# Decode attention with a gated unit: loading Wq as 16 partitions and then 112, instead of a quarter of every partition's rows and then the rest

## The chip, the cores and the metric

The kernel runs on one core of a Trainium2 chip. The metric is the device time of one execution in microseconds, and the number that counts is the median of several runs. One more execution was taken with the hardware profiler; it has a span (first to last recorded instruction) and a device time of its own that is a little longer than the span.

## The reference, cut to what matters

Everything is bfloat16 in memory. There are 8 sequences of one new token each (B = 8, D = 512), 32 query heads, 8 key/value heads of 128 elements, and a cache of 8192 positions of which the last W = 2048 are attended to.

```python
xn = layernorm(x)                                  # (8, 1, 512)
q  = (xn @ wq)                                     # wq: (512, 4096) -> 32 heads x 128
k  = k_cache[:, :, Sk - W:, :]                     # (8, 8, 2048, 128), each head for 4 q heads
v  = v_cache[:, :, Sk - W:, :]
p  = softmax(q . k * 128 ** -0.5)
s  = (p . v) @ wo                                  # wo: (4096, 512)
h  = sigmoid(xn @ w_gate) * (xn @ w_up)            # w_gate, w_up: (512, 1792)
g  = silu(h @ w_down)                              # w_down: (1792, 512)
return x + s * g
```

The windows of K and V are 4 MB for each sequence, Wq and Wo are 4 MB each, and the three matrices of the gated unit are 1.75 MB each: some 81 MB are read and 8 KB written.

## The kernel before, in words

Every large operand is loaded into a ring of five buffers of 32 KB per partition (`ring_tile`), each of which holds one 4 MB operand. The loads stand in a list, `loads`, in the order Wq, K0, K1, K2, V0, then K and V alternating, then the gate and up matrices, the down matrix, and Wo. `issue_loads` takes loads off the list while `free_bufs` says that a buffer is free. All of them are issued from SyncE (SP). The first five are issued at once; each later one is issued where the program has read a buffer out, and waits on SP until that is so. The order of all other work is written out by hand (`manual_schedule`), and each engine follows it.

Wq is seen as 128 partitions of KT = 4 rows: partition p holds rows 4p to 4p + 3, each 4096 elements (8 KB), so that a partition's 32 KB lie in one piece in memory and in the buffer. `load_wq` (lines 96 to 103) issues two loads at line 101.

Meanwhile x is loaded from ScalarE's queue, normalised on VectorE and transposed into `xnT_sb`. The q matmuls (line 303) go over the halves s, then over kt, then over four column strips a:

```python
for kt in range(KT):
    for a in range(QP):
        nc.tensor.matmul(q_ps[PW * a : PW * (a + 1), :],
                         lhsT=xnT_sb[:, kt, :],
                         rhs=w_tiles["q"][:, kt, o : o + rep * Dh], ...
```

Each contracts over all 128 partitions of Wq. VectorE copies the result to `qx_sb` (L313) and transposes it (L322), TensorE spreads it (L330), ScalarE copies it to `qc_sb` (L338), and `q_fill` (L349) puts 16 small copies per sequence into the operand `qz`. When q has been read out of Wq, that buffer is handed to the load of K3.

For each sequence b, VectorE transposes the K tile in four turns (`k_turn`, L371), TensorE makes the scores (`qk`, L388), and the softmax and the product with V follow one or two sequences later (L401 to L544). The gated unit and the product with Wo (L668) stand at the end, Wo in seven loads that grow smaller so that little is left to do after the last one.

## Time and profile before

| | |
|---|---|
| median of 3 runs | 197.53 us (197.53 to 197.66) |
| the profiled execution: device time | 197.59 us |
| the profiled execution: span | 195.8 us |
| PE matmul busy | 114.0 us (58%), 1092 instructions |
| DVE busy | 116.8 us (60%), 170 instructions |
| ACT busy | 38.7 us (20%), 112 instructions |
| POOL busy | 7.5 us (4%), 27 instructions |
| loads on the one queue | 6368 packets, 81.01 MB, 97.3% of 16 engines' span |
| HBM reads over the span | 414 GB/s |
| from issue to landing: first piece of Wq, second piece | 4.8 us, 11.6 us |
| from issue to landing: K, V (median) | 29.4 us, 24.1 us |
| mean granted TensorE clock | 0.808 |

The busy times of the compute engines are sums over the span; the line for loads is the time that packets took on the 16 DMA engines together. "Issue to landing" counts from the instruction on SP to the completion of the whole load, and so takes in the time that the load stands behind others in the queue.

### The profile page before, as it was taken

The page shows a single profiled execution, that of the slowest core. Times are in us where ns is not written, and L with a number is a line of the kernel's source. Part 1 is how long each engine was busy: PE and PEld are TensorE (multiplying, and loading weights), DVE is VectorE, ACT ScalarE, POOL GpSimd, SP SyncE. Part 2 cuts the span into 40 slices and gives each one's busy share as a digit, 9 for nine tenths or more (in the row PEclk, how much of TensorE's full clock was granted, in tenths as well). Part 3 has the DMA queues.
Part 4 walks back from the last instruction along what each step waited for, and adds up shares of the span by engine and source line. Part 5 has one row for each costly group of instructions (what it writes and reads, how often), then busy time and mean ns, then how long its engine had stood idle before and what let it go on. Part 6 is the DMA issues. An engine that isn't in the chain of part 4 may idle for free.

```text
span 195.8 us, 2620 instructions
## 1 busy us (share of the span) xinstructions
PE 114.0 (58%) x1092; PEld 47.6 (24%) x1092; DVE 116.8 (60%) x170; ACT 38.7 (20%) x112; POOL 7.5 (4%) x27
## 2 busy tenths in 40 slices
PE   0133025709709970799059923990796099687562
PEld 0011001102103240214021311160225025463461
DVE  2304498299398449944895479739936952454101
ACT  1102910015015011501141003211501110225000
POOL 2480000000000000000000000000000000000000
PEclk9999555855975998599958995798599579969699
DMA  6999999999999999999999999999999999999991
GB/s 241 457 402 432 429 442 432 432 429 429 429 429 429 429 432 437 425 424 429 432 435 429 429 435 439 432 429 425 432 429 432 425 429 439 422 428 426 421 398 39
DMA packets 6410, 81.17 MB, mean 415 GB/s; under 512 B 1000, under 2 KB 1024, under 8 KB 1408
## 3 DMA queue, kind: packets, MB, share of 16 engines
q1 hardware_dynamic: 6368, 81.01, 97.3%
q8 instruction: 8, 0.13, 0.2%
q10 hardware_dynamic: 32, 0.01, 0.0%
q14 instruction: 2, 0.02, 0.0%
HBM read 81.01 MB, written 0.01 MB: 414 GB/s over the span
## 4 chain that ended last, share of the span: by engine, by line
DMA 33%; PE 32%; DVE 30%; issue 1%; ACT 1%; SPq 1%; DVEq 0%
PE s_ps L388 24%; DVE k_sb L371 24%; DMA wo_sb<-in_A_wo_dram 11%; DMA v_sb<-in_A_v_cache_dram 11%; DMA k_sb<-in_A_k_cache_dram 11%; PE o_ps L493 6%; DVE o_r L514 2%; DVE pt_bf L433 2%; PE o_ps L522 1%; DVE o_sb L544 1%; ACT o_r L510 1%; DVE o_q L535 1%; DVE mx L401 1%; SPq L101 0%; PE pc_ps L439 0%
## 5 line engine op out<-in xcount | busy, mean ns | idle before, releaser
L371 DVE STREAM_TRANSPOSE k_sb<-k_sb 128x2048 uint32<-128x2048 uint32 x32 | 72.9, 2292 | 6.1 <-DMA k_sb<-in_A_k_cache_dram 6.0
L388 PE MATMUL s_ps<-k_sb,qz 128*32 128x512 bf16 x256 | 61.7, 1086 | 11.7 <-DVE k_sb L371 11.6
L439 PE MATMUL pc_ps<-pt_bf,spr 128*32 128x128 bf16 x128 | 4.7, 292 | 40.8 <-DVE pt_bf L433 40.8
L401 DVE TENSOR_REDUCE mx<-s_ps 128x1 f32<-128x512 f32 x8 | 5.5, 692 | 28.7 <-PE s_ps L388 28.7
L493 PE MATMUL o_ps<-v_sb,pT_sb 128*32 128x256 bf16 (+1 forms) x416 | 22.0, 310 | 0.0
L388 PEld LDWEIGHTS <-qz 128*32 128x32 bf16 x256 | 10.0, 114 | 48.7 <-issue 48.6
L493 PEld LDWEIGHTS <-pT_sb 128*32 128x32 bf16 (+1 forms) x416 | 14.7, 105 | 14.7 <-issue 9.7
L349 ACT COPY qz<-qc_sb 32x64 bf16<-32x64 bf16 x64 | 16.5, 303 | 0.7
L510 ACT ACTIVATE o_r<-o_ps,Cm 128x128 f32<-128x128 f32 x16 | 5.9, 368 | 53.3 <-PE o_ps L493 53.3
L514 DVE SCALAR_TENSOR_TENSOR o_r<-o_ps,Cm,o_r 128x128 f32<-128x128 f32 x28 | 9.7, 350 | 10.6 <-ACT o_r L510 10.2
L420 ACT ACTIVATE p_bf<-s_ps,nm 128x512 bf16<-128x512 f32 x8 | 5.5, 687 | 49.8 <-DVE nm L417 49.8
L439 PEld LDWEIGHTS <-spr 128*32 128x32 bf16 x128 | 3.4, 121 | 41.5 <-issue 40.9
L522 PE MATMUL o_ps<-o_r,rows 128*128 128x128 f32 x32 | 7.9, 339 | 4.8 <-DVE o_r L514 4.8
L475 DVE TENSOR_SCALAR pT_sb<-pc_bf,quarter 128x512 bf16<-128x512 bf16 x32 | 9.0, 350 | 0.2 <-ACT pc_bf L449 0.2
L449 ACT CAST pc_bf<-pc_ps 128x512 bf16<-128x512 f32 x8 | 4.7, 586 | 20.3 <-PE pc_ps L439 20.3
L303 PE MATMUL q_ps<-wq_sb,xnT_sb 128*32 128x512 bf16 x32 | 3.7, 611 | 5.4 <-DMA wq_sb<-in_A_wq_dram 5.0
L522 PEld LDWEIGHTS o_ps<-o_r,rows 128*128 128x128 f32 x32 | 5.1, 206 | 6.7 <-DVE o_r L514 6.7
L668 PE MATMUL a_ps<-wo_sb,o_sb 128*32 128x128 bf16 x128 | 4.7, 222 | 2.7 <-DMA wo_sb<-in_A_wo_dram 2.6
L433 DVE STREAM_TRANSPOSE pt_bf<-p_bf 128x512 bf16<-128x512 bf16 x8 | 5.4, 675 | 0.9 <-ACT p_bf L420 0.9
L535 DVE SCALAR_TENSOR_TENSOR o_q<-o_ps,rden,block 128x128 f32<-128x128 f32 x8 | 2.8, 351 | 5.2 <-PE o_ps L522 5.2
L313 DVE CAST qx_sb<-q_ps 128x256 bf16<-128x256 f32 x4 | 1.5, 420 | 7.0 <-PE q_ps L303 7.0
L668 PEld LDWEIGHTS <-o_sb 128*32 128x32 bf16 x128 | 4.0, 98 | 3.8 <-issue 3.7
(62 smaller groups left out, 54.6 us busy)
## 6 DMA issues: line engine op xcount, KB each, us to landing
k_sb<-in_A_k_cache_dram SPq DMA_DIRECT2D x8, 4096.0 KB, 29.4
v_sb<-in_A_v_cache_dram SPq DMA_DIRECT2D x7, 4096.0 KB, 24.1
v_sb<-in_A_v_cache_dram SPq DMA_DIRECT2D x2, 2048.0 KB, 19.9
wq_sb<-in_A_wq_dram SPq DMA_DIRECT2D x1, 3072.0 KB, 11.6
wgu_sb<-in_B_w_gate_dram SPq DMA_DIRECT2D x1, 1792.0 KB, 25.1
wgu_sb<-in_B_w_up_dram SPq DMA_DIRECT2D x1, 1792.0 KB, 28.9
wd_sb<-in_B_w_down_dram SPq DMA_DIRECT2D x1, 1792.0 KB
wo_sb<-in_A_wo_dram SPq DMA_DIRECT2D x1, 1408.0 KB
```

The lines of the kernel that those rows point to most:

```text
L349: nc.scalar.copy(out=z[rows, GL * gg : GL * (gg + 1), :, c0 : c0 + rep], in_=qc_sb[rows, :, gg, :, :, b].rearrange("p gl r we -> p gl we r"),)
L371: nc.vector.transpose(out=words, in_=words)
L388: nc.tensor.matmul(s_tiles[b][PW * gl : PW * (gl + 1), :], lhsT=qz[b % 2][:, h, we, :], rhs=kv[:, gg, gl, we // 2, we % 2], start=(we == 0 ...
L401: nc.vector.reduce_max(out=mx[:], in_=s_tiles[b][:], axis=AX.X)
L433: nc.vector.transpose(out=pt_bf[:].rearrange("p c g a r -> p (c g a r)"), in_=p_bf[:])
L439: nc.tensor.matmul(pc_ps[PW * a : PW * (a + 1), cl], lhsT=spr[:, cl].rearrange("k p gl -> k (p gl)"), rhs=pt_bf[:, :, :, a, :], start=True ...
L475: nc.vector.tensor_scalar(out=pT[:, :, :, gl, :], in0=pc[:].rearrange("p c g r -> p g c r"), scalar1=quarter[:, gl : gl + 1], scalar2=None ...
L493: nc.tensor.matmul(o_ps[rows * cg : rows * (cg + 1), :], lhsT=pT_tiles[b][:, gg, nch * m : nch * (m + 1)].rearrange("p c g r -> p (c g r)" ...
L510: nc.scalar.activation(out=o_r[:], in_=o_ps[:, 0:Dh], func=AF.Copy, scale=cm[:, 0:1])
L514: nc.vector.scalar_tensor_tensor(out=o_r[:], in0=o_ps[:, Dh * c : Dh * (c + 1)], scalar=cm[:, c : c + 1], in1=o_r[:], op0=ALU.mult, op1=AL ...
L522: nc.tensor.matmul(o2_ps[:], lhsT=rows128[gg][:].rearrange("p gl g r q -> p (gl g r q)"), rhs=o_r[:], start=(gg == 0), stop=(gg == NG - 1),)
L668: nc.tensor.matmul(a_ps[s][32 * c : 32 * (c + 1), :], lhsT=o2_sb[:, m, :], rhs=w_tiles["o"][:, m, DC * c + HC * s : DC * c + HC * (s + 1)] ...
```

## The change

Wq is still loaded by two loads from SP, in front of all others. Before, the first load brought row kt = 0 of every partition (128 packets of 8 KB, 1 MB in all) and the second rows 1 to 3 (128 packets of 24 KB, 3 MB). Now the first brings all four rows of partitions 0 to 15 (16 packets of 32 KB, 512 KB) and the second all four rows of partitions 16 to 127 (112 packets of 32 KB, 3.5 MB). Nothing else differs: all engines have the same instructions in the same order, two lines further up in the file after this place.

```diff
         src = A_wq.rearrange("(p kt) n -> p kt n", kt=KT)
-        for k0, k1 in ((0, 1), (1, KT)):
-            nc.sync.dma_start(
-                out=w_tiles["q"][:, k0:k1, :], in_=src[:, k0:k1, :]
-            )
+        for p0, p1 in ((0, 16), (16, P)):
+            nc.sync.dma_start(out=w_tiles["q"][p0:p1], in_=src[p0:p1])
```

## The prediction

> **What bounds the kernel now.** I read the page's slices first, then the queue totals, the chain in order of time, and last the first 32 us by timeline and by quarter-microsecond windows. From the page, the 40 slices of 4.9 us (busy tenths of the 16 DMA engines, then what they moved) and the queue that carries the loads (packets, MB, share of 16 engines' span):

> ```profile
> DMA  6999999999999999999999999999999999999991
> GB/s 241 457 402 432 429 442 432 432 429 429 429 429 429 429 432 437 425 424 429 432 435 429 429 435 439 432 429 425 432 429 432 425 429 439 422 428 426 421 398 39
> ...
> q1 hardware_dynamic: 6368, 81.01, 97.3%
> ```

> All loads go through one queue, and apart from the first slice and the last it never runs dry: 81.01 MB at some 430 GB/s is 188 us of a 195.8 us span. From the chain in order of time (start us, us, what), its first and last parts:

> ```profile
> 1.20 0.41 SPq L101
> 1.60 0.05 issue
> 1.66 20.83 DMA k_sb<-in_A_k_cache_dram
> ...
> 147.15 0.55 SPq L114
> 147.69 0.05 issue
> 147.75 22.01 DMA v_sb<-in_A_v_cache_dram
> 169.75 0.02 issue
> 169.77 22.31 DMA wo_sb<-in_A_wo_dram
> 192.08 0.04 issue
> ```

> The chain passes through DVE and PE between these, but the last V loads land 22 us after their issue: about 9.5 MB go through the queue in that time, their own 2 MB among them. So the engines of the core follow the stream, and its end follows its own bytes. Time lost on the DMA engines near the start is lost at the end, to the full amount; a delay off that stream costs nothing until its slack is used up.

> The start, in windows (us, busy time of PE, PEld, DVE, ACT, POOL, granted clock, DMA share, GB/s):

> ```profile
> 1.50:1.75 0.25, 0.00 (x0) 0.00 (x0) 0.00 (x0) 0.00 (x0) 0.25 (x2) 1.00 0.09 29
> 1.75:2.00 0.25, 0.00 (x0) 0.00 (x0) 0.00 (x0) 0.00 (x0) 0.13 (x1) 1.00 1.95 299
> 2.00:2.25 0.25, 0.00 (x0) 0.00 (x0) 0.00 (x0) 0.00 (x0) 0.00 (x0) 1.00 1.01 164
> 2.25:2.50 0.25, 0.00 (x0) 0.00 (x0) 0.00 (x0) 0.00 (x0) 0.00 (x0) 1.00 0.43 164
> 2.50:2.75 0.25, 0.00 (x0) 0.00 (x0) 0.02 (x1) 0.00 (x0) 0.00 (x0) 1.00 0.61 197
> 2.75:3.00 0.25, 0.00 (x0) 0.00 (x0) 0.25 (x1) 0.00 (x0) 0.00 (x0) 1.00 0.87 360
> 3.00:3.25 0.25, 0.00 (x0) 0.00 (x0) 0.22 (x2) 0.00 (x0) 0.00 (x0) 1.00 1.01 426
> ```

> Bytes flow 1 us after the first issue at 0.73 and reach full rate at 3.0. From 1.75 to 3.0 they come to (299 + 164 + 164 + 197 + 360) x 0.25 = 296 KB where 432 GB/s would have brought 540 KB: the slow start loses 0.56 us.

> **The change, part by part.** Bytes, issues and order are the same: two loads of Wq, then K0, K1, K2, V0. The packets differ: 128 of 8 KB and 128 of 24 KB become 16 of 32 KB and 112 of 32 KB. Per DMA engine that is one packet, then seven, instead of eight and eight. The unit: 432 GB/s (the rate between 40 and 80 us) over 16 engines is 27.0 GB/s for each, so a 32 KB packet takes 1.21 us.

> *The head of 16 partitions.* Every large load in the trace writes all 128 partitions, so the trace doesn't tell whether 27 GB/s is what one DMA engine sends or what one set of eight partitions can take. If only the engine limits, 512 KB takes 1.21 us and the head costs nothing. If the sets limit, 16 partitions reach at least two of the 16 sets: 54 GB/s, 9.7 us, which is 8.5 us more. With four sets it is 108 GB/s and 4.85 us, with eight 2.43 us. I take four: 4.85 us lies between the geometric (3.4) and the arithmetic middle (5.5) of the two ends. **Cost +3.64 us**, ends 0 and +8.5.

> [...]

> *The other 112 partitions.* Seven rows for each of 16 engines. The engines' own time is 7 x 1.21 = 8.5 us, the remaining seven eighths of Wq, so without meetings it costs nothing. But blocks of seven rows don't line up with sets of eight: where sets limit, two engines meet on one set at some steps and each takes double. Ends: no meetings, 0; a meeting at every step, +8.5 us. Since K0 lands when the slowest engine has delivered, and every later load gives each engine an equal share, the slowest engine's lag stays to the end. I take the middle, **+4.2 us**, for the row lies near neither end: engines start in step on blocks seven rows apart, then drift.

> *The slow start.* The worst windows still moved 164 to 197 GB/s, more than the 108 that the head can take, so the slow start now hides behind the head: **-0.56 us**. If it doesn't hide, 0.

> *The early matmuls.* Four q matmuls of kt=0 now run before the second piece lands; after the change every q matmul reads all 128 partitions and waits for both loads. The rows, from the timeline between 7 and 28 us (start us, us):

> ```profile
> 7.18 0.62 PE L303 MATMUL q_ps<-wq_sb,xnT_sb 128*32 128x512 bf16 x4 [0.34 <-DVE xnT_sb L205]
> ...
> 12.81 3.06 PE L303 MATMUL q_ps<-wq_sb,xnT_sb 128*32 128x512 bf16 x28 [5.01 <-DMA wq_sb<-in_A_wq_dram]
> ...
> 19.68 4.11 ACT L349 COPY qz<-qc_sb 32x64 bf16<-32x64 bf16 x16
> 22.51 6.70 DVE L371 STREAM_TRANSPOSE k_sb<-k_sb 128x2048 uint32<-128x2048 uint32 x3 [4.55 <-DMA k_sb<-in_A_k_cache_dram]
> ...
> 27.07 1.13 PE L388 MATMUL s_ps<-k_sb,qz 128*32 128x512 bf16 x4 [8.37 <-DVE k_sb L371]
> ```

> They put 0.62 us behind Wq's landing. The path from q ends with the copies into qz at 23.79, and the first matmul that reads them starts at 27.07, released by the transposes of K0: 3.28 us of slack. Wq and K0 are delayed alike, so the slack stays and the cost is **0**; without that cover it is 0.62 us.

> *SP.* Still two issues at L101, 0.41 us each; K0 to V0 queue behind them as now. The load of K3 waits until q has been read, issued at 15.91 now and at about 24 then. K0, K1, K2 and V0 (16.8 MB, 39 us) are queued ahead of it, so it stays covered. Later issues move with the landings. A lag of one engine by 4.2 us is within the shortest lead of the last loads (14.3 us from issue to landing), so no engine runs dry. **0**; nothing is late next but the stream.

> Sum: 3.64 + 4.2 - 0.56 = +7.3 us on the profiled execution's 197.59 us (span 195.8 and 1.8 around it; the median of the runs is 197.53): **204.9 us**.

> **The rivals.**

> *Head only.* The sets limit, but 112 rows flow as evenly as 128. For it: 112 rows still reach every set, and engines that fall out of step may stay out of each other's way. Against: blocks of seven and sets of eight share no alignment. 197.59 + 3.64 - 0.56 = 200.7 us.

> *Faster: only the engines limit.* The slow start is then a cost of the first packets: now 128 of 8 KB, each 32 KB from the next in Wq, then one run of 512 KB in 16 packets. For it: the loss sits wholly in the first 1.25 us, in which the first 8 KB packets flow. Against: a load on cold queues would begin as slowly with any packet, and then nothing changes. If the first 32 KB packets flow at 432 GB/s, 0.56 us goes: 197.0 us. It decides if the first piece lands under 1.8 us after its first byte.

> *Two sets.* Adjacent partitions share a set in blocks of eight: 197.59 + 8.5 + 4.2 - 0.56 = 209.7 us.

> *Strided rows.* If the 112 rows are dealt to the engines one by one, every step is again 16 adjacent rows: eight steps of +3.64, less 0.56, gives 226 us. For it: nothing in the trace tells how rows are dealt. Against: the even 430 GB/s of loads with eight rows per engine, which a deal of that kind couldn't reach if sets limit.

> **How the numbers follow.** Forecast 0.50; head only 0.24; engines only 0.12 (a gain 0.07, no difference 0.04, slightly slower 0.01); two sets 0.08; strided 0.06. A measurement of this kernel tells about 0.2% (0.4 us) from no change. The range runs from 200.0, below the head alone, to 210.0, above two sets; it leaves out engines only, strided, and the fringes. Faster 0.07, same 0.04, slower 0.89.

> **What would show it.** In the windows of the changed kernel, the DMA should move some 110 GB/s from about 1.75 to 6.5 us (full rate there would prove the head wrong), then below 430 until some 18 us. K0's first transpose should start near 30 instead of 22.51; a start near 26 means no meetings, one at 22 that only engines limit. From 40 us on the rate should be 430 again, with the last wo landing late by as much as K0. If K0 is late and the end isn't, the stream isn't the bound.

## The result and the profile after

The changed kernel takes 206.76 us (median of 5 runs, 206.49 to 206.96) against 197.59 us of the kernel before on the same chip: a ratio of 1.046, interval 1.045 to 1.047, or 9.2 us more. Its profiled execution took 206.77 us with a span of 205.0 us.

The slices of the profile's page are now 5.1 us long. These are the busy tenths of the 16 DMA engines, the rate, and the queue of the loads:

```profile
DMA  7999999999999999999999999999999999999991
GB/s 117 205 294 240 368 448 422 435 432 419 451 409 448 422 438 432 416 436 420 448 422 441 422 428 438 422 441 422 432 432 432 432 422 438 422 436 422 422 384 32
...
q1 hardware_dynamic: 6240, 81.01, 97.2%
```

The bytes are the same, with 128 packets fewer. The DMA engines count as busy from the first slice on, as before, but in the first five slices, some 25 us, they move far less. "Busy" here means that packets are open; the lower rate tells that each of them takes longer (2.17 us against 1.21, below). From the sixth slice on everything flows as before (409 to 451 GB/s up to the last two slices). The chain in order of time, its first and last parts:

```profile
1.18 0.40 SPq L101
1.58 0.05 issue
1.63 30.25 DMA k_sb<-in_A_k_cache_dram
...
177.51 23.15 DMA wo_sb<-in_A_wo_dram
200.66 0.04 issue
200.70 0.62 PE a_ps L666 x16
```

K0 lands after 30.25 us instead of 20.83, 9.4 us later, and the end moves nearly as much, by 9.2 us. The last row of the chain, the addition that makes y, before and after:

```profile
193.14 0.28 DVE y_bf L686
```

```profile
202.37 0.28 DVE y_bf L684
```

The DMA issues give the landing of the two pieces of Wq (KB, us from issue to landing); they were issued at 0.73 and 1.18:

```profile
wq_sb<-in_A_wq_dram SPq DMA_DIRECT2D x1, 3584.0 KB, 21.1
...
wq_sb<-in_A_wq_dram SPq DMA_DIRECT2D x1, 512.0 KB, 6.7
```

So the head lands at 7.4 us and the 112 other partitions at 22.3. The windows count a packet's bytes where the packet starts, so a short window is lumpy when packets last 2 to 4 us (801 GB/s from 1.50 to 2.00 us, 66 from 2.00 to 4.00). Here are two windows that hold several packets of each engine (start and end, length in us, busy times, granted clock, DMA share, GB/s):

```profile
8.20:20.00 11.80, 0.00 (x0) 0.00 (x0) 0.37 (x2) 0.00 (x0) 5.93 (x16) 1.00 1.00 261
24.00:32.00 8.00, 3.08 (x24) 0.99 (x17) 2.86 (x6) 2.93 (x10) 0.00 (x0) 1.00 1.01 434
```

The 112 partitions flow at 261 GB/s, K0 behind them at 434. In the packet records of the trace the 16 packets of the head take 3.1 to 4.0 us. Those of the 112 take a median of 2.17 us, where 1.21 us is the full rate. Taken in order of start as seven rounds of 16, they have medians of 2.73, 2.20, 1.75, 1.61, 2.03, 2.18 and 2.12 us, and not one packet takes less than 1.60: all engines are slow, not a few.

The path from q, from the timeline:

```profile
22.46 3.60 PE L301 MATMUL q_ps<-wq_sb,xnT_sb 128*32 128x512 bf16 x32 [15.23 <-DMA wq_sb<-in_A_wq_dram]
...
30.08 4.12 ACT L347 COPY qz<-qc_sb 32x64 bf16<-32x64 bf16 x16
31.90 8.89 DVE L369 STREAM_TRANSPOSE k_sb<-k_sb 128x2048 uint32<-128x2048 uint32 x4 [3.75 <-DMA k_sb<-in_A_k_cache_dram]
...
36.46 1.12 PE L386 MATMUL s_ps<-k_sb,qz 128*32 128x512 bf16 x4 [7.15 <-DVE k_sb L369]
```

All 32 q matmuls now wait for the second piece. The copies into qz end at 34.20 and the first matmul that reads them starts at 36.46. The transposes of K0 still release it, so 2.26 us of slack are left of 3.28.

### The profile page after: what moved, and what is told of

Same layout as the page of the kernel before. It is cut to its first block, busy times and chain, and to the rows that moved or that the text cites. A ratio compares the mean times of both kernels' runs of the same rounds, so it can differ in the third digit from the quotient of the medians.

```text
span 205.0 us, 2621 instructions
## 1 busy us (share of the span) xinstructions
PE 114.4 (56%) x1092; PEld 48.0 (23%) x1092; DVE 116.7 (57%) x170; ACT 38.6 (19%) x112; POOL 7.5 (4%) x27
## 3 DMA queue, kind: packets, MB, share of 16 engines
q1 hardware_dynamic: 6240, 81.01, 97.2%
HBM read 81.01 MB, written 0.01 MB: 395 GB/s over the span
## 4 chain that ended last, share of the span: by engine, by line
PE 36%; DVE 34%; DMA 26%; issue 1%; ACT 1%; SPq 1%; DVEq 0%
DVE k_sb L369 27%; PE s_ps L386 26%; DMA k_sb<-in_A_k_cache_dram 15%; DMA wo_sb<-in_A_wo_dram 11%; PE o_ps L491 8%; DVE pt_bf L431 2%; DVE o_r L512 2%; PE o_ps L520 1%; DVE o_sb L542 1%; ACT o_r L508 1%; DVE o_q L533 1%; DVE mx L399 1%; PE a_ps L666 1%; SPq L146 0%; SPq L101 0%
## 5 line engine op out<-in xcount | busy, mean ns | idle before, releaser
L491 PE MATMUL o_ps<-v_sb,pT_sb 128*32 128x256 bf16 (+1 forms) x416 | 23.2, 324 | 0.0
L386 PEld LDWEIGHTS <-qz 128*32 128x32 bf16 x256 | 10.5, 114 | 47.0 <-issue 46.9
L491 PEld LDWEIGHTS <-pT_sb 128*32 128x32 bf16 (+1 forms) x416 | 15.2, 109 | 15.1 <-issue 9.8
L311 DVE CAST qx_sb<-q_ps 128x256 bf16<-128x256 f32 x4 | 1.5, 420 | 16.8 <-PE q_ps L301 16.8
L336 ACT CAST qc_sb<-qr_ps 128x512 bf16<-128x512 f32 x2 | 1.1, 588 | 22.8 <-PE qr_ps L328 22.8
```

Of the source, the lines that this page charges most:

```text
L386: nc.tensor.matmul(s_tiles[b][PW * gl : PW * (gl + 1), :], lhsT=qz[b % 2][:, h, we, :], rhs=kv[:, gg, gl, we // 2, we % 2], start=(we == 0 ...
L491: nc.tensor.matmul(o_ps[rows * cg : rows * (cg + 1), :], lhsT=pT_tiles[b][:, gg, nch * m : nch * (m + 1)].rearrange("p c g r -> p (c g r)" ...
```

## Experiments

All experiments change `load_wq` alone; their times stand beside runs of the kernel before on the same chip (197.5 to 197.7 us).

### Which side is slow: the partitions written or the memory read

Theory S supposes that the partitions written share a limited way in, theory H that adjacent rows of memory share a limited way out. The changed kernel can't tell them apart, since its rows are adjacent on both sides. Four kernels load Wq in eight loads of 16 rows, adjacent or eight apart on either side. Where the two sides differ, rows land in other partitions than they should; the work stays the same:

```diff
-        for p0, p1 in ((0, 16), (16, P)):
-            nc.sync.dma_start(out=w_tiles["q"][p0:p1], in_=src[p0:p1])
+        far = src.rearrange("(j r) kt n -> r j kt n", r=8)
+        for r in range(8):
+            # e1: out [16 * r : 16 * (r + 1)], in src[16 * r : 16 * (r + 1)]
+            # e2: out [16 * r : 16 * (r + 1)], in far[r]
+            # e3: out [r : P : 8],             in src[16 * r : 16 * (r + 1)]
+            # e4: out [r : P : 8],             in src[r : P : 8]
```

> Wq comes in eight loads of 16 partitions; each writes 16 adjacent partitions and reads 16 adjacent rows of 32 KB of memory, as the changed kernel's first load does. In the changed kernel that load held the DMA engines for about 4 us (from 1.76 us to between 5 and 6.3) where 1.21 us was its share. Both theories expect eight times this: some 32 to 36 us for Wq instead of 9.7, and a time of 220 to 224 us. Theory S (the partitions written limit) and theory H (the memory read limits: adjacent rows of 32 KB lie in too few parts of it) differ only in the next three kernels. If instead the 4 us were a cost of the cold start, the other seven loads take 1.2 us each and the time is about 200 us.

> Eight loads of 16 adjacent partitions, but each reads 16 rows that lie 256 KB apart in memory, so the rows of Wq land in other partitions than they should (the output is not the reference's; the work is the same). Theory S: as slow as with adjacent rows, 220 to 224 us. Theory H: the reads are spread, the loads run at full rate, and the time is 197.5 to 198.5 us.

> Eight loads that read 16 adjacent rows each and write 16 partitions that lie eight apart (rows land in other partitions than they should, so the output is not the reference's). Theory S: partitions eight apart reach more sets; with eight sets a load takes 2.4 us, Wq 19.4 us, and the time is about 207 us; with all 16 sets 197.5 to 198.5. Theory H: 220 to 224 us, as with adjacent partitions.

> Eight loads of 16 partitions eight apart, from the rows of memory that belong to them, 256 KB apart. Theory S: the same time as with adjacent rows and partitions eight apart, about 207 us (eight sets). Theory H: 197.5 to 198.5 us.

| partitions written | rows read | time | one packet, median behind the first 16 |
|---|---|---|---|
| adjacent | adjacent | 223.9 us | 4.60 us |
| adjacent | eight apart | 223.0 us | 4.36 us |
| eight apart | adjacent | 208.2 us | 2.54 us |
| eight apart | eight apart | 208.3 us | 2.54 us |

Theory S holds in so far as the side written decides: the rows read change the time by under 1 us, the partitions written by 15 to 16. The window of the first kernel over five rounds of packets, and that of the third over seven:

```profile
9.90:32.90 23.00, 0.00 (x0) 0.00 (x0) 0.00 (x0) 0.00 (x0) 4.27 (x10) 1.00 1.01 114
```

```profile
4.00:21.60 17.60, 0.29 (x4) 0.31 (x5) 1.91 (x8) 1.35 (x2) 6.18 (x17) 1.00 1.01 209
```

Sixteen adjacent partitions take 114 GB/s, close to a quarter of 430, and partitions eight apart 209, close to half. The seven loads behind the first are as slow as was expected of the head (4.60 us a packet), so the head's loss isn't a cost of the cold start.

### One load, two halves, and the order

```diff
-        for p0, p1 in ((0, 16), (16, P)):
-            nc.sync.dma_start(out=w_tiles["q"][p0:p1], in_=src[p0:p1])
+        # e6: nc.sync.dma_start(out=w_tiles["q"], in_=src)
+        # e7: the loop over ((0, 64), (64, P))
+        # e8: the loop over ((0, 112), (112, P))
```

> Wq in one load of 128 partitions, 32 KB each. Theory S (the partitions reached by the engines at one time limit, not the size of a packet): full rate from the start, no head and no meetings, 197.0 to 197.8 us. If the slow start of the kernel before is a cost of its 8 KB packets, 197.0 to 197.2; if it is a cost of any first packet, 197.4 to 197.8. If 32 KB packets were slow in themselves, it would take 5 us or more longer.

> Wq as partitions 0 to 63 and then 64 to 127. By theory S each half reaches half of the 16 sets, two engines on each: packets of 2.3 to 2.5 us, Wq in about 20 us, a time of 207.5 to 208.5 us as with 16 partitions eight apart. If only loads of fewer rows than engines times two are slow, or engines take their rows so that they don't meet, 197.5 to 198 us.

> The two loads in the other order and at the other end: partitions 0 to 111 first, then 112 to 127. The sum of the two terms doesn't depend on the order: 206 to 207.5 us, with packets of about 2.1 us first and 16 packets of about 4.6 us behind them. If the loss of the 112 came from engines that left the head out of step, they flow at 1.2 us now, and the time is about 201 to 202 us.

One load of 128 packets of 32 KB takes 197.80 us, ratio to the kernel before 1.001 (1.0002 to 1.002), or 0.27 us more: the size of a packet costs next to nothing, and nothing is won either. Its window behind the first packets:

```profile
3.70:12.20 8.50, 0.29 (x4) 0.30 (x5) 1.92 (x8) 1.57 (x2) 4.91 (x16) 1.00 0.99 428
```

Packets behind the first 16 take 1.21 us, the first 16 a median of 1.90. So the slow start is there with large packets too, and the time is at the upper end of what was expected.

The halves take 208.4 us with packets of 2.56 us, as expected of two engines on each set. The other order, 112 before 16, takes 206.7 us, as much as the changed kernel. The landings (KB, us from issue to landing; issued at 0.73 and some 1.18):

```profile
wq_sb<-in_A_wq_dram SPq DMA_DIRECT2D x1, 3584.0 KB, 17.8
wq_sb<-in_A_wq_dram SPq DMA_DIRECT2D x1, 512.0 KB, 21.4
```

The 112 land at 18.5 and the 16 adjacent ones at 22.6, 4.1 us later. The packets of the 16 took 3.2 to 4.4 us, a little under the 4.6 expected; those of the 112 behind their first round took a median of 2.0 us. So the loss of the 112 is there without a head in front of them, and doesn't come from engines that left the head out of step.

### How the 112 rows are dealt to the engines

```diff
-        for p0, p1 in ((0, 16), (16, P)):
-            nc.sync.dma_start(out=w_tiles["q"][p0:p1], in_=src[p0:p1])
+        nc.sync.dma_start(out=w_tiles["q"][0:16], in_=src[0:16])
+        for j in range(7):
+            nc.sync.dma_start(out=w_tiles["q"][16 + j : P : 7], in_=src[16 + j : P : 7])
```

> The first load is the changed kernel's (16 adjacent partitions); the 112 others come in seven loads of 16 partitions that lie seven apart (16, 23, 30, ... then 17, 24, ...), one packet per DMA engine and load. That is the order in which the engines would work if the one load of 112 were dealt as a block of seven adjacent rows to each engine. Theory C (blocks of seven, whose meetings on a set cost the time): the same as the changed kernel, packets of about 2.1 us after the first, 206 to 207.5 us. Theory D (the 112 rows are dealt in another way): another time; if a load of 16 partitions seven apart meets no other on its sets, 1.2 us each and 201 us; if pairs meet all the time, 2.5 us each as with partitions eight apart, 209 to 210 us.

It took 207.0 us with a median packet of 2.19 us (2.17 in the changed kernel). Its window, beside the 261 GB/s of the changed kernel:

```profile
8.20:20.00 11.80, 0.00 (x0) 0.00 (x0) 0.45 (x3) 0.00 (x0) 6.01 (x17) 1.00 1.05 267
```

Its seven loads have median packets of 2.76, 2.24, 1.86, 1.75, 1.97, 2.22 and 2.13 us, nearly the rounds of the one load of 112. That is theory C: seven loads whose rows are placed by hand as blocks of seven do what the one load of 112 does. Dealing row by row, one of the rivals, is what the first kernel above does, and is far slower (223.9 us).

### Where a load of 64 partitions begins

If rows come in blocks, a load of 64 partitions gives engine e the partitions p0 + 4e to p0 + 4e + 3. Sliding p0 changes which partitions are written at the same time. By theory S two engines meet when the partitions that they write share a way in; which ones do, no run shows. "Coupled" below stands for the case that a meeting slows all 16 engines, not only those that meet.

```diff
-        for p0, p1 in ((0, 16), (16, P)):
+        # e9:  ((32, 96), (0, 32), (96, P))
+        # e10: ((28, 92), (0, 28), (92, P))
+        # e12: ((24, 88), (0, 24), (88, P))
+        # e11: ((16, 80), (0, 16), (80, P))
```

> Wq as partitions 32 to 95 first, then 0 to 31, then 96 to 127. With blocks of adjacent rows per DMA engine, the first load has engine e at partition 32 + 4e at its first step. [...] Wq in 4 x 1.2 + 4 x 2.5 = 15 us, a time of 202.5 to 203.5 us. Rival B (sets are eight adjacent partitions, with some other rate): 64 adjacent partitions reach eight sets wherever they begin, packets of 2.5 us, 208 to 209 us as with the halves.

> The same shifted by four: partitions 28 to 91 first, then 0 to 27 and 92 to 127. [...] The two loads behind it have 28 and 36 rows, which don't divide by 16, so the whole time says little: 205 to 213 us.

> Partitions 16 to 79 first, then 0 to 15, then 80 to 127. [...] Coupled: all packets of the first load take 2.2 to 2.5 us. [...] Behind it 16 adjacent partitions (4.6 us) and 48 in three packets of some 3 us: Wq in some 23 us and 209 to 212 us when coupled.

> Partitions 24 to 87 first, then 0 to 23 and 88 to 127. [...] The loads behind it have 24 and 40 rows, so the whole time says little: 208 to 216 us.

The middle 64 took 203.2 us, inside the 202.5 to 203.5 expected; that the first load would run at full rate was an assumption of the author's, which no run before it showed. Eight adjacent partitions as a set (208 us) are out. Here is the first load of each kernel, in a window behind its cold first packets, with the start at partition 32, 28, 24 and 16:

```profile
3.80:7.60 3.80, 0.29 (x4) 0.21 (x4) 1.74 (x8) 1.52 (x2) 0.38 (x3) 1.00 0.97 414
```

```profile
3.80:7.60 3.80, 0.29 (x4) 0.21 (x4) 1.74 (x8) 1.52 (x2) 0.38 (x3) 1.00 0.99 388
```

```profile
4.00:9.20 5.20, 0.29 (x4) 0.21 (x4) 1.92 (x8) 1.21 (x2) 1.97 (x9) 1.00 1.02 208
```

```profile
3.90:9.10 5.20, 0.29 (x4) 0.21 (x4) 1.92 (x8) 1.49 (x2) 1.70 (x7) 1.00 1.01 208
```

With the start at 28 most packets keep 1.21 to 1.25 us, and a few take 2.4 to 2.5, twice as long; the others aren't slowed with them. With the start at 24 all 16 engines take 2.5 to 2.6 us a packet, no less than at 16 or, in the halves, at 0. So in these kernels the cost doesn't grow step by step as the start moves down: it jumps between 28 and 24. Which engines meet in each of these loads, and how many, isn't shown.

The whole times (212.7, 217.7 and 214.4 us with the start at 28, 24 and 16) hold the loads behind, whose packets took up to 4.7 us. With the start at 28 and at 24 the engines also seem to have ended apart: the next to last slice fell to 296 and 269 GB/s, from 398 in the kernel before. What each of these adds isn't shown. At 24 and at 16 the time was above the 208 to 216 and 209 to 212 expected, at 16 because the 48 last partitions took some 3.9 us a packet and not 3.

Two things stay open. If the one load of 128 partitions gave each engine eight adjacent rows, its engines would write partitions eight apart at every step, as the loads of 16 partitions eight apart did at 209 GB/s, and yet it runs at 428. So either its rows are dealt in another way than those of 112 and 64, or the partitions written aren't all that counts; no run here takes that apart. And the third and fourth round of the 112 (medians 1.75 and 1.61 us) lie between the 1.21 us of full rate and the 2.5 to 2.6 of the slow first loads; why isn't shown.

## Why the prediction was right, and where it was not

It said 204.9 us (200 to 210); 206.76 came. The path, the head and the kind of loss of the 112 were as forecast; the size of one term was not. By its steps:

- **The bound.** Right. Lost DMA time goes to the end nearly in full: K0's first transpose is 9.4 us later (31.90 against 22.51, where a start near 30 was forecast), the final addition 9.2 us, and the queue holds 434 GB/s as soon as Wq is through.
- **The head, +3.64 less 0.56 for the hidden start.** Right, though "four sets" was picked as a middle between two ends and not read from a row, which is partly luck. With one load Wq lands at 13.0 us (12.3 after 0.73); seven rounds of 1.21 us back from there, its first round, slow start and all, landed at about 4.6 us. The head landed at 7.4: 2.9 us more, where 3.08 was forecast. Behind a warm queue a packet takes 4.60 us where four sets gave 4.85. Eight such loads at 3.39 us above the full rate, less 0.56 once, would come to 26.6 us; the first of the four kernels lost 26.3. How many sets 16 partitions reach, and that there are sets of eight at all, no run shows; what the runs show is 114 GB/s for 16 adjacent partitions, where four sets gave 108.
- **The 112, +4.2.** That they lose was right, and the blocks of seven placed by hand (2.19 us a packet against 2.17) fit the account of it; the size was not right. From 7.4 to 22.3 us is 14.9 us against 8.5: 6.4 us. The step that failed is the middle between "no meetings" and "a meeting at every step", and with it the notion that two engines that meet lose time, the slowest lags and the others run ahead. Not one of the 112 packets took less than 1.60 us, and in the first loads that begin at 24 and 16 all 16 engines take 2.5 to 2.6. So here the engines lose time together, and it is three quarters of the upper end (6.4 of 8.5 us). Which engines meet in which round isn't shown, so the single rounds (2.73 down to 1.61 us) and with them the account of the size stay in part open. The 2.2 us that the term lacked are most of the miss of the sum; the head's 0.2 us the other way leave some 1.9.
- **The slow start as a gain.** The rival on the faster side fell: one load with 32 KB packets starts as slowly and takes 197.80 us.
- **The early matmuls.** Cost 0, as forecast, but the slack didn't stay whole: 2.26 us of 3.28. Wq's second piece landed 9.5 us later and K0 9.4, and the head start of the four early matmuls was lost on top.
- **SP.** Right: K3 was issued at 26.11 us (about 24 forecast), and no slice behind shows a gap in the stream.
- **The other rivals.** Head only (200.7) fell with the 14.9 us that the 112 took. Two sets (209.7) fell with 4.60 us a packet, strided rows (226) with the blocks of seven.

## What to carry to other kernels

On this queue Wq did best in loads of all 128 partitions: in one load (428 GB/s, 197.80 us) or, if a part is wanted early, cut along the free dimension, as the kernel before did (197.5 us). Every cut along the partitions that was tried cost 5.5 us or more, even where the second part was large. And a DMA share of 1.00 says that packets are open, not that bytes flow: read the GB/s beside it (1.00 stood beside 261, 1.01 beside 434).

## What had not been expected of the hardware

- A first load of 64 partitions that begins at 28 left most packets at 1.21 to 1.25 us, a few at 2.4 to 2.5; beginning at 24, four partitions lower, all 16 engines took 2.5 to 2.6 us. Why isn't settled.
- Sixty-four partitions run at full rate if they are 32 to 95 (414 GB/s) and at half if they are 0 to 63 (packets of 2.56 us).
- Rows far apart in memory gave 4.36 us a packet against 4.60 for adjacent ones where the partitions written were adjacent, and 2.54 either way where they were eight apart: in the slowest case a small part of the time hangs on the side read after all.
